# A chunk pair's added state products moved ahead of a tile of hidden products, with a filler behind them

## The chip, the cores and the metric

The kernel runs on one core of one Trainium2 chip. The metric is device time in microseconds, the median of several executions of the same program. Three executions of the kernel before took 361.55, 362.46 and 362.59 us.

## The reference

Two stages run one after the other. The first is a state-space recurrence over 768 tokens for 4 batches of 8 heads, with a state of 16 x 32 per head. In chunked form:

```
for each chunk:
    y_intra = ((C B^T) * L) x            # L: products of a, causal
    y_inter = (C state) * decay_to_i
    state   = decay_full * state + sum_j decay_from_j * B_j x_j
```

The sum in the last line is what this kernel calls the added products. The second stage takes y as 3072 tokens of 256 features through two layers with a leaky slope per hidden feature:

```
h = y @ w_in                              # 256 -> 2048
g = max(h, 0) + alpha * min(h, 0)
out = g @ w_out                           # 2048 -> 256
```

Everything is float32, except that the two weight matrices reach the kernel as float64 words, which it converts on the chip.

## The kernel before, in words

Tokens are taken in chunks of 128, two chunks making a pair, 12 pairs in all; four chunks make a group of 512 tokens for the second stage. The order of all work is written by hand: each engine runs its instructions in the order in which the code issues them, and waits for semaphores where a tile is not ready or not free.

The change lies in the start, `first_two()` (from line 816), which does the recurrence of pairs 0 and 1 while weights are still loaded and converted. It uses half chunks of 64 tokens. The steps of pair 1 that matter, with their lines:

- B and C of pair 1 are transposed on TensorE by `turned` (line 838), two transposes of B into one bank of PSUM, two of C into another; ScalarE copies both to SBUF, C first (line 840). `spread_c` (line 847, ScalarE) makes two masked copies of C, `decayed_c` (line 954, GpSimd) a decayed one.
- `scan` (line 864, VectorE) makes the decays, four of them, reading banks 0 to 3 of PSUM (`sp`).
- `added` (line 888, TensorE, 16 matmuls of 64 x 32, which are 32 records in the profile) makes the added products from `bn1` (B scaled, made on GpSimd at line 528) and `xt1` (x of pair 1, loaded by DMA at line 196). It writes the right-hand halves of the two banks `own`.
- `states` (line 903, VectorE) turns them into states, and `one_at_a_time` masks those on GpSimd (line 909).
- `gram_of` (line 874, TensorE) makes C B^T in banks 0 to 3, right-hand halves, and `times` (line 880, VectorE) multiplies it with the decays.
- `x_products` (line 922) and `state_products` (line 934) make y on TensorE, which `copy_out` (lines 942 and 943) brings to SBUF.

Beside these runs the second stage for group 0. `hidden_two` (line 1092) makes two tiles of hidden products for 256 tokens in one bank: four matmuls, two per tile, for the tile and half of the input features. It takes a function `after`, which is called behind each of the four and issues other work there; in `first_two` this is `among(i, k)`. So the added products stand behind the first of the four matmuls, gram behind the second, and the products of x and of the states behind the third. The four read columns 256 to 511 of w_in, the third and fourth tile of 128 hidden features. These columns are the second piece of w_in, whose conversion ends on GpSimd at line 327. Pair 0's y is their other operand.

`keep_warm` (line 335) issues fillers: matmuls of ones whose results nobody reads. There are four calls of it before the changed place.

Two banks are called `hp` (pool `ps_h`), two `ss` (`ps_s`), and four are named by number (`ps_q`). `second` is one of the `hp` banks; C's transposes go to it, and afterwards the tile of `hidden_two`.

Of the kernel before, what the change touches and what calls it, by code (L numbers as in the profile page):

```python
# [22 lines left out]
def kernel(  # L23
# [80 lines left out]
    def bank(i):  # L104


        return ps_q.tile([P, 512], F32, name="bank", tag=f"q{i}")
# [180 lines left out]
    def sign(dst, src, sg):  # L288

        if src.dtype == F32 or id(dst) in signs:  # L290
            return
        r = wtp.tile([P, 2, WQ], U32, name="wr")
        nc.vector.tensor_single_scalar(out=r, in_=parts[id(dst)][0], scalar=SIGN,
                                       op=ALU.bitwise_and)
        signs[id(dst)] = r
# [36 lines left out]
    def keep_warm(to, n, cols=2 * Q):  # L332

        for i in range(n):
            nc.tensor.matmul(to[:, :cols], warm.to_broadcast([P, P]), warm.to_broadcast([P, cols]),
                             start=True, stop=True, skip_group_check=True)
# [53 lines left out]
    def slope_signs():  # L390
        if moe_w_out.dtype == F32:
            nc.vector.tensor_single_scalar(out=s_out, in_=s_mul.bitcast(U32), scalar=SIGN,
                                           op=ALU.bitwise_and)
        else:
            for o, by in ((g_mul, 2.0**-11), (g_add, 2.0**25)):
                nc.gpsimd.tensor_scalar(out=o, in0=s_mul, scalar1=by, scalar2=None, op0=ALU.mult)
# [119 lines left out]
    def pair_loads(gp):  # L516

        b, c = divmod(2 * gp, CPB)
        nat, abc, xt, ap = loads["p", gp]

        bn = work.tile([P, 2, H * N], F32, name="bn")
        i, bi = divmod(b, 2)
        if gp >= HALF:
            pj = prt[i].rearrange("p (j b m h) -> p j b m h", j=2, b=2, h=H)[:, :, bi, c // 2]
        else:
            pj = (prt[i if gp >= NB else "short"]
                  .rearrange("p (b h c) -> p b c h", b=2, h=H)[:, bi, c : c + 2])
        nc.gpsimd.tensor_tensor(
            out=bn.rearrange("p k (h n) -> p k h n", h=H),
            in0=nat[:, 0].rearrange("p k (h n) -> p k h n", h=H),  # L530
            in1=pj.unsqueeze(3).to_broadcast([P, 2, H, N]), op=ALU.mult)
        return bn
# [8 lines left out]
    def spare():  # L541

        return ps_h.tile([P, GT], F32, name="hp", tag="hp")
# [272 lines left out]
    def first_two():  # L816
# [15 lines left out]
        def turned(nat, banks):  # L832


            bc = work.tile([P, 4, Q], F32, name="bc")
            for i, tp in enumerate(banks):
                for k in range(2):
                    nc.tensor.transpose(tp[:, k * P : (k + 1) * P], nat[:, i, k], ident)
            for i in (1, 0):
                nc.scalar.copy(out=bc[:, 2 * i : 2 * i + 2].rearrange("p k t -> p (k t)"),  # L840
                               in_=banks[i][:, : 2 * Q])
            return bc

        def spread_c(bc):
            cz = czp.tile([P, 2, 2, Q], F32, name="cz")
            for e in range(2):
                nc.scalar.mul(cz[:, e].rearrange("p k t -> p (k t)"),
                              bc[:, 2:].rearrange("p k t -> p (k t)"), par[:, e : e + 1])
            return cz
# [17 lines left out]
        def gram_of(bc, cz, banks):  # L867
            for v in range(2):
                for k in range(2):
                    for r in (2 * v, 2 * v + 1):  # L870
                        rs = slice(32 * r, 32 * r + 32)
                        for j, hs in enumerate(halves):
                            o = banks[r][hs, (2 + k) * Q : (3 + k) * Q]
                            nc.tensor.matmul(o.rearrange("p (e t) -> p e t", e=2), bc[rs, k, hs],
                                             cz[rs, :, k, hs], start=True, stop=True,
                                             tile_position=(32 * r, HQ * j),
                                             skip_group_check=True)

        def times(i, r, t):
            nc.vector.tensor_tensor(out=dec[i][:, r], in0=t[:, 2 * Q :], in1=dec[i][:, r],  # L880
                                    op=ALU.mult)

        def added(dps, bn, xt):
            for k in range(2):
                for r in range(4):
                    rs = slice(32 * r, 32 * r + 32)
                    for j, hs in enumerate(halves):
                        nc.tensor.matmul(dps[j][rs, k], bn[hs, k, rs],
                                         xt[hs, k, 2 * r * D : 2 * (r + 1) * D],
                                         start=True, stop=True, tile_position=(HQ * j, 32 * r),  # L890
                                         skip_group_check=True)

        def dps_in(banks):
            return [t[:, 2 * Q : 2 * Q + 4 * D].rearrange("p (k m) -> p k m", k=2) for t in banks]

        def states(i, dps, pf, cs=range(4)):
            for c in cs:
                if i == 0 and c == 0:
                    nc.scalar.copy(out=new[0][:, 0], in_=dps[0][:, 0])
                    continue  # L900
                e = (c + 1) * HQ - 1
                old = new[i][:, c - 1] if c else new[0][:, 3]
                nc.vector.scalar_tensor_tensor(out=new[i][:, c], in0=old, scalar=pf[:, e : e + 1],
                                               in1=dps[c % 2][:, c // 2], op0=ALU.mult,
                                               op1=ALU.add)

        def mask(i, cs):
            n = cs.stop - cs.start
            nc.gpsimd.tensor_tensor(
                out=sm[i][:, cs].rearrange("p k (g m) -> p k g m", g=2),  # L910
                in0=new[i][:, cs].unsqueeze(2).to_broadcast([P, n, 2, 2 * D]),
                in1=hmask.rearrange("p (g m) -> p g m", g=2).unsqueeze(1)
                .to_broadcast([P, n, 2, 2 * D]), op=ALU.mult)
# [24 lines left out]
        def copy_out(i, y):  # L938
            for w in range(KC):
                o = xts[0][:, w, 2 * i * Q : 2 * (i + 1) * Q].rearrange(  # L940
                    "p (k j t) -> p j k t", k=2, j=2)
                nc.scalar.copy(out=o[:, 0], in_=y[w][0])
                nc.scalar.copy(out=o[:, 1], in_=y[w][1])

        def places(first, second):
            return [[t[:, :Q].rearrange("p (k t) -> p k t", k=2) for t in ts]
                    for ts in (first, second)]

        def ss():
            return ps_s.tile([P, 512], F32, name="ss")  # L950

        def decayed_c(bc, pf):
            cd = work.tile([P, 2, Q], F32, name="cd")
            nc.gpsimd.tensor_tensor(out=cd.rearrange("p k t -> p (k t)"),
                                    in0=bc[:, 2:].rearrange("p k t -> p (k t)"), in1=pf,
                                    op=ALU.mult)
            return cd

        def one_at_a_time(i, cs):
            for c in cs:  # L960
                mask(i, slice(c, c + 1))
# [9 lines left out]
        sp = [bank(r) for r in range(4)]  # L971
# [5 lines left out]
        nat1, _, xt1, pf1 = loads["p", 1]  # L977
# [13 lines left out]
        dps = dps_in([hp, tp])  # L991
# [18 lines left out]
        sp = [bank(r) for r in range(4)]  # L1010
# [16 lines left out]
        bn1 = pair_loads(1)  # L1027
        convert_next(first=False)
        own = [ss(), ss()]
        second = spare()  # L1030
        bc1 = turned(nat1, (own[0], second))
        cz1 = spread_c(bc1)
        dps = dps_in(own)
        mask(0, slice(3, 4))
        slope_signs()
        cd1 = decayed_c(bc1, pf1)

        def among(i, k):
            if (i, k) == (0, 0):
                added(dps, bn1, xt1)  # L1040
                states(1, dps, pf1, range(3))
                one_at_a_time(1, range(3))
            if (i, k) == (0, 1):
                gram_of(bc1, cz1, sp)
                for r in range(4):
                    times(1, r, sp[r])
                states(1, dps, pf1, (3,))
                prelu_of[0]()
                convert_a(*pieces[2])
                sign(*pieces[2])  # L1050
            if (i, k) == (1, 0):
                y = places([own[0], bank(0)], [bank(1), bank(2)])
                x_products(y, xt1, 1)
                state_products(y, 1, cd1)
                copy_out(1, y)
# [507 lines left out]
```

## Time and profile before

| | us |
|---|---|
| median of three executions | 362.46 |
| lowest and highest | 361.55, 362.59 |
| the profiled execution, its own time | 361.22 |
| span of the profiled execution, first to last instruction | 359.5 |
| TensorE busy (products) | 352.6 (98%) |
| VectorE busy | 239.6 (67%) |
| GpSimd busy | 202.2 (56%) |
| ScalarE busy | 172.3 (48%) |
| mean granted clock of TensorE | 0.991 |
| TensorE waiting for the conversion of w_in, line 1092, longest | 1.2 |
| TensorE waiting at line 922, releaser "issue" | 1.1 |
| VectorE waiting for the added products, line 903 | 1.0 |

A busy TensorE is not TensorE at its peak, since products are pipelined and their ends are modelled. The profile names, for each idle stretch of an engine, what ended it: another engine's instruction, a DMA, or "issue", which means that the engine waited for nothing that the profile shows. A float32 matmul shows as two records, a transpose as one. The granted clock is the share of full speed that TensorE's clock had. Windows give, for a stretch of time, the busy microseconds of each engine and that clock. The chain of waits is followed back from the last instruction, and tells which engine's work set the end.

### The profile page before, as it was taken

Reading aid. Unit: us, or ns where it says so; the run is one execution under the profiler, and the core shown is the slowest. Engines: PE = TensorE matmul, PEld = TensorE weight load, DVE = VectorE, ACT = ScalarE, POOL = GpSimd, SP = SyncE. Lnnn points to the kernel's source line nnn. Section 1 sums busy time; section 2 is a strip of 40 time slices with the busy share of each in tenths; the row PEclk is TensorE's granted clock in tenths of the full one; section 3 lists DMA queues with packets and bytes.
Section 4 is the critical chain, followed back from the end, with each engine's and each line's share of the span. In section 5 each row is a group of like instructions: output and inputs, shape, how many; then the busy total and the mean of one; then the engine's idle time right before and its main releaser. Section 6 shows DMA issues by size and latency. Waiting matters only on the chain.

```text
span 359.5 us, 7769 instructions
## 1 busy us (share of the span) xinstructions
PE 352.6 (98%) x2981; PEld 286.4 (80%) x2981; DVE 239.6 (67%) x483; ACT 172.3 (48%) x391; POOL 202.2 (56%) x227
## 2 busy tenths in 40 slices
PE   8889999999999999999999999999999999999996
PEld 3567566668888888888888888888888888888885
DVE  6966996999947856866656856657856634643363
ACT  3537666535354445445345445445545444443431
POOL 6653748579847947536546536537536545434510
PEclk9988999999999999999999999999999999999999
DMA  8999999205436502502522521531201001001102
GB/s 149 189 211 339 253 282 204 77 2 116 131 86 145 110 3 60 116 3 49 101 61 51 94 64 43 97 69 42 34 2 31 0 2 29 2 1 29 33 0 58
DMA packets 105581, 30.24 MB, mean 84 GB/s; under 512 B 79896, under 2 KB 101448, under 8 KB 105544
## 3 DMA queue, kind: packets, MB, share of 16 engines
q1 hardware_dynamic: 103048, 29.43, 35.6%
q10 hardware_dynamic: 2496, 0.32, 0.6%
q8 instruction: 23, 0.38, 0.4%
q14 instruction: 14, 0.11, 0.1%
HBM read 26.32 MB, written 3.42 MB: 83 GB/s over the span
## 4 chain that ended last, share of the span: by engine, by line
PE 96%; DMA 1%; DVE 1%; issue 0%; POOL 0%; SPq 0%; ACT 0%; POOLq 0%
PE bank L1198 33%; PE hp L1223 28%; PE bank L1124 8%; PE hp L1077 6%; PE ss L1223 6%; PE hp L1092 2%; PE ss L782 1%; PE ss L726 1%; DMA nat<-in_B_dram 1%; PE bank L1191 1%; PE ss L800 1%; PE ss L774 1%; PE ss L737 1%; PE bank L1092 1%; PE ss L613 1%; PE ss L934 0%
## 5 line engine op out<-in xcount | busy, mean ns | idle before, releaser
L1280 POOL TENSOR_TENSOR gt<-gt 128x512 f32<-128x512 f32 x58 | 74.2, 1278 | 21.1 <-DVE gt L1208 16.3
L1198 PE MATMUL bank<-gt,w_out 128*128 128x256 f32 x320 | 83.5, 381 | 0.0
L1198 PEld LDWEIGHTS bank<-gt,w_out 128*128 128x128 f32 x320 | 60.1, 190 | 9.2 <-issue 1.0
L1208 DVE SCALAR_TENSOR_TENSOR gt<-hp,s_mul,gt 128x256 f32<-128x256 f32 x96 | 42.0, 479 | 29.1 <-ACT gt L1206 26.8
L1270 POOL TENSOR_TENSOR gt<-gt 128x512 f32<-128x512 f32 x20 | 25.4, 1269 | 62.6 <-DVE gt L1208 49.8
L1206 ACT ACTIVATE gt<-hp,s_alpha 128x256 f32<-128x256 f32 x96 | 40.3, 471 | 34.6 <-PE hp L1223 31.5
L1198 PE MATMUL bank<-gt,ws 128*128 128x256 f32 x224 | 55.9, 379 | 0.0
L1198 PEld LDWEIGHTS bank<-gt,ws 128*128 128x128 f32 x224 | 42.3, 190 | 5.6
L1223 PE MATMUL hp<-xs,w_in 128*128 128x256 f32 x160 | 41.9, 384 | 0.0
L1223 PE MATMUL hp<-xs,ws 128*128 128x256 f32 x160 | 41.2, 380 | 0.0
L1249 DVE TENSOR_TENSOR hp<-hp,u 128x512 f32<-128x512 f32 x20 | 14.0, 700 | 35.2 <-ACT u L1247 35.2
L1223 PEld LDWEIGHTS hp<-xs,ws 128*128 128x128 f32 x160 | 30.3, 190 | 4.3 <-POOL xs L1165 0.2
L1223 PEld LDWEIGHTS hp<-xs,w_in 128*128 128x128 f32 x160 | 29.7, 190 | 4.5
L1124 PE MATMUL bank<-w_out,gt 128*128 128x256 f32 x128 | 31.0, 384 | 0.0
L1124 PEld LDWEIGHTS bank<-w_out,gt 128*128 128x128 f32 x128 | 23.6, 190 | 6.5 <-issue 2.9
L1223 PE MATMUL ss<-xT,w_in 128*128 128x256 f32 x96 | 24.6, 379 | 0.0
L1077 PE MATMUL hp<-xT,w_in 128*128 128x512 f32 x48 | 22.7, 595 | 0.0
L556 DVE TENSOR_TENSOR_SCAN dec<-abc,bank 128x192 f32<-128x192 f32 x48 | 22.7, 523 | 0.0
L640 POOL TENSOR_TENSOR sm<-state,bmask 128x256 f32<-128x256 f32 (+1 forms) x10 | 6.2, 619 | 28.9 <-DVE state L637 28.9
L1238 ACT COPY m<-hp 128x512 f32<-128x512 f32 x8 | 4.7, 586 | 35.7 <-PE hp L1223 35.7
L1247 ACT COPY u<-hp 128x512 f32<-128x512 f32 x20 | 11.7, 585 | 19.4 <-PE hp L1223 19.4
L1208 DVE SCALAR_TENSOR_TENSOR gt<-c,s_mul,gt 128x256 f32<-128x256 f32 x40 | 20.6, 555 | 0.0
(230 smaller groups left out, 615.8 us busy)
## 6 DMA issues: line engine op xcount, KB each, us to landing
abc<-z SPq DMA_DIRECT2D x24, 192.0 KB
raw<-in_moe_w_in_dram SPq DMA_DIRECT2D x8, 512.0 KB
raw<-in_moe_w_out_dram SPq DMA_DIRECT2D x8, 512.0 KB
abc<-z SPq DMA_DIRECT2D x8, 512.0 KB
out_dram<-o_sb SPq DMA_DIRECT2D x32, 64.0 KB
nat<-in_B_dram SPq DMA_DIRECT2D x26, 64.0 KB
xt<-in_x_dram SPq DMA_DIRECT2D x12, 128.0 KB
xt<-in_x_dram SPq DMA_DIRECT2D x24, 64.0 KB
```

What stands on the lines that cost most here:

```text
L556: nc.vector.tensor_tensor_scan(out=dv[:, o : o + SQ], data0=abc[k][:, s : s + SQ], data1=ident_p[0][:, :SQ], initial=0.0, op0=ALU.mult, op ...
L1077: nc.tensor.matmul(hp, w_in[:, k, f * P : (f + 1) * P], xts[g][:, k], start=(k == 0), stop=(k == KC - 1))
L1092: nc.tensor.matmul(hp[:, i * nt : (i + 1) * nt], w_in[:, k, fs], xts[g][:, k, ts], start=(i == 0 and k == 0), stop=(k == KC - 1), skip_gro ...
L1124: nc.tensor.matmul(pos[0][t // 2][:, t % 2], gt[:, t * Q : (t + 1) * Q], w_out[:, f], start=(f == 0 and t % 2 == 0), stop=(f == NF - 1), s ...
L1198: nc.tensor.matmul(ms[g][i][:, h], w, blocks[g, z][n][:, p], start=(q == 0 and h == 0), stop=(q == NQ - 1), skip_group_check=True)
L1206: nc.scalar.mul(o[:, p], h[:, p], s_alpha[:, fs[p]])
L1208: nc.vector.scalar_tensor_tensor(out=o[:, p], in0=h[:, p], scalar=s_mul[:, fs[p]], in1=o[:, p], op0=ALU.mult, op1=ALU.max)
L1223: nc.tensor.matmul(to[:, p], w(2 * z + p), b, start=start and p == 0, stop=True, skip_group_check=True)
L1247: nc.scalar.copy(out=u2, in_=A)
L1249: nc.vector.tensor_tensor(out=Y, in0=Y, in1=u2, op=ALU.add)
L1270: nc.gpsimd.tensor_tensor(out=tc_, in0=g22, in1=g12, op=ALU.subtract)
L1280: eng.tensor_tensor(out=o, in0=x0, in1=x1, op=ALU.subtract)
```

## The change

Two things are changed, both in `first_two`, and one is added:

```diff
         own = [ss(), ss()]
         second = spare()
-        bc1 = turned(nat1, (own[0], second))
+        bc1 = turned(nat1, (sp[0], second))
         cz1 = spread_c(bc1)
         dps = dps_in(own)
         mask(0, slice(3, 4))
         slope_signs()
         cd1 = decayed_c(bc1, pf1)
+        added(dps, bn1, xt1)
+        states(1, dps, pf1, range(3))
+        one_at_a_time(1, range(3))
+        keep_warm(second, 1)

         def among(i, k):
-            if (i, k) == (0, 0):
-                added(dps, bn1, xt1)
-                states(1, dps, pf1, range(3))
-                one_at_a_time(1, range(3))
             if (i, k) == (0, 1):
                 gram_of(bc1, cz1, sp)
```

B of pair 1 is transposed into bank 0, which the first scan has read, instead of a bank of `own`. The added products, three of the four state updates and their masks are issued in front of the tile's first matmul instead of behind it. One filler of 256 columns is issued between the added products and the tile, into the bank that the tile takes next. On VectorE, ScalarE, GpSimd and SyncE the instructions keep their order. On TensorE the added products and the filler stand behind the transposes, and the tile's first two matmuls stand together; the program has one matmul more.

## Prediction

> **What bounds the kernel now.** I read the chain of waits first, then the 40 slices, then TensorE's timeline and one-microsecond windows around the moved step. The chain is TensorE for 96% of the span, so only time that TensorE gains or loses counts. Of the slices, one row matters:
>
> ```profile
> PEclk9988999999999999999999999999999999999999
> ```
>
> The granted clock is full except in the third and fourth slice (18 to 36 us), just behind the changed step. The timeline of TensorE there (start, duration, engine, line, tiles, count; the bracket is the idle time before it and what ended it):
>
> ```profile
> 16.29 0.38 PE L838 MATMUL hp<-ident,nat 128*128 128x128 f32 x2
> 17.87 0.70 PE L1092 MATMUL hp<-xT,w_in 128*128 128x256 f32 x2 [1.20 <-POOL w_in L327]
> 18.50 0.46 PE L888 MATMUL ss<-xt,bn 64*32 64x64 f32 x32
> 18.89 0.70 PE L1092 MATMUL hp<-xT,w_in 128*128 128x256 f32 x2
> 19.52 0.72 PE L874 MATMUL bank<-cz,bc 32*64 32x128 f32 x32
> 20.17 0.70 PE L1092 MATMUL hp<-xT,w_in 128*128 128x256 f32 x2
> ...
> 23.05 0.41 PE L922 MATMUL bank<-dec,xt 64*32 64x64 f32 x20 [1.05 <-issue]
> ```
>
> See two holes. The first, 1.20 us, waits for GpSimd's conversion of the second piece of w_in (16.55 to 17.81). The second, 1.05 us, stands inside the products of L922 and is released by "issue": nothing that the profile shows. After it the clock falls (windows: length, then busy time and counts of TensorE, weight loads, VectorE, ScalarE, GpSimd, then clock, DMA share, GB/s):
>
> ```profile
> 22.00:23.00 1.00, 0.00 (x0) 0.00 (x0) 0.94 (x3) 0.00 (x0) 0.00 (x0) 1.00 0.91 137
> 23.00:24.00 1.00, 0.95 (x28) 0.86 (x28) 0.90 (x3) 0.00 (x0) 0.11 (x1) 0.77 1.20 113
> 24.00:25.00 1.00, 1.00 (x12) 1.00 (x12) 1.00 (x2) 0.13 (x1) 1.00 (x1) 0.50 1.10 188
> 29.00:30.00 1.00, 1.00 (x3) 0.78 (x3) 0.62 (x1) 0.14 (x1) 0.23 (x1) 0.50 1.00 307
> 30.00:31.00 1.00, 1.00 (x5) 0.86 (x4) 0.27 (x1) 0.70 (x2) 1.00 (x1) 0.82 0.98 354
> ```
>
> Windows of 0.1 us put the fall at 23.57 and the return at 30.36: 6.79 us at half clock, some 3.4 us lost. So three things lie near the change: a hole that it fills, a hole that it does not touch, and a throttle.
>
> **What the Trainium skill says.** (1) "TensorE: Matmul & The Clock Gate", Part 1: the clock is halved or full, decided by how busy TensorE was in windows of about 3.4 us. The trace agrees in kind: 0.50 or 1.00, and 6.79 us is two such windows. (2) "Runtime: NRT & Kernel Launch", Instruction fetch mechanics: an engine's instructions are refilled in blocks of 256 (16 KiB), by a DMA queue of the sequencer's own. The page of before fits:
>
> ```profile
> q8 instruction: 23, 0.38, 0.4%
> ```
>
> That is 23 packets of 16 KB; 6041 TensorE instructions in the built program make 23.6 blocks. The 1.05 us hole stands after 706 of them (346 products and 346 weight loads in the windows up to 23.0, and 14 others in the program); 62 that run ahead of the program would put it on 3 x 256 (the 62 is inferred). One packet of this queue begins at 20.57 and lasts 1.04 us (6.5% of 16 engines over 20 to 21 us), so it ends at 21.6, and TensorE goes on at 23.05. I read the hole as a late instruction block. The block before ended at instruction 450, at 13.98, so the request is that old; from then on the 16 DMA engines were full (share 0.97 to 1.34 in each microsecond from 14 to 21). (3) "PSUM — Partial Sum Buffer", PSUM bank collisions: a bank may not be written by TensorE while another engine reads it. In the trace L888 comes only after both copies of L840 have ended (17.35).
>
> **The change part by part.** Sums are made against the profiled execution: 361.22 us, span 359.5, 1.7 around it; it stands 1.24 below the median 362.46 of the three timed runs (361.55 to 362.59). A difference carries over to the median.
>
> *B's transposes go to bank 0.* Same two instructions. They must wait for VectorE's scan of that bank, over at 14.14, against 16.07 when they run; ScalarE's copy (16.97) waits for the same scan. Cost nothing. The gain is that the added products need not wait for ScalarE's copies.
>
> *The added products (32 matmul records, L888) move ahead of the tile, into the first hole.* They need bn, made by 15.40, and pair 1's x, whose DMAs were issued from 13.44 to 14.65. Its landing isn't shown; before, L888 at 18.50 did not wait for it. Early end: they run at 16.7, right behind the transposes. Late end: 18.5. I take 16.7 to 17.1, since the DMA engines had moved some 345 KB from 13.4 to 16.2, more than the 320 KB of C and x.
>
> *The filler, one 256-column product into the bank of the tile.* A lone one costs 0.70 (L335 at 13.37). It waits for ScalarE's copy of C, 16.71 to 17.08, and so ends at about 17.8, as the conversion does (17.81): it costs 0 to 0.1, hidden by GpSimd. If x lands at 18.5, it and L888 delay the tile by 1.7 us.
>
> *TensorE then:* first product of the tile at 17.87, as before, since GpSimd still bounds it. Its second product follows back to back: 0.70 + 0.43 (two records at 0.216, as L1124's eight in 1.73 on the chain) instead of 0.70 + 0.39 + 0.63, saving 0.59. Gram, the third product: 17.87 + 1.13 + 0.65 + 0.63 = 20.28, where before it was 20.87.
>
> *VectorE:* the three state updates of L903 waited 0.95 for L888 and ran 19.13 to 20.11; now they follow the scans at 18.17 and end at 19.15. The order of VectorE's queue stays, so nothing is put behind a new wait. The four products of L880 (1.42) no longer start at 20.22 but when half of gram is done, 19.0 + 0.33 + 0.1, and end at 20.85 instead of 21.64. Nor do GpSimd's masks (L909) get later. SyncE's queue and all DMAs stay.
>
> *Where it goes:* L922 starts at 20.28 and no longer stops for VectorE. 42 of its 64 records, at 0.41/20 each as in the row at 23.05, take it to the block's end: 21.1 instead of 21.99, so TensorE is 0.9 us early at the second hole. Three instructions more ahead of L922 move that end by two records, nothing else. But the block it waits for was requested at 13.98, before the first instruction that moves, and sits behind DMAs issued before 17.5, which the change doesn't touch. So it should arrive at 23.05 all the same. What is late next is the fetch: the hole grows from 1.05 to about 2.0 us and swallows the 0.9. Even the late end of x (L922 at about 22) is mostly covered by it.
>
> *From 23.05 on* nothing is new: 22 records instead of 20 (0.04), the state products, the copies, the last product of the tile, and eleven to twelve products at half clock if the throttle stays. Sum: about 0, which gives 362.4.
>
> **Rivals.**
> 1. *The hole moves with TensorE* (it isn't a DMA's landing, or the fetch comes earlier): -0.9, 361.6. For: "issue" names no releaser. Against: its place on 256 instructions, the packet at 20.57.
> 2. *The clock doesn't fall.* The filler and L888 fill a hole of 1.2 us within the 6.8 us before the fall (16.74 to 23.57). Avoided whole, it gives half of 6.79: -3.4, 359.1; cut to one window, -1.7, 360.7. For: the filler is a full-width product, and 16.74 to 20.15 was only 2.28 of 3.41 us busy. Against: the later window, 20.15 to 23.57, was 2.35 of 3.42 us busy and gets emptier, about 1.5, by my own account of the hole.
> 3. *Slower: the clock falls a window earlier or returns a window later,* because of that emptier window. 3.4 us more at half clock cost up to 1.7: 364.1; half that where part of it lies in the hole. It decides once the window up to 23.57, or one that straddles the hole otherwise, is too empty for the clock to come back after the next: of 3.4 us the hole would take 2.0. Against: L922 and the state products are short and would cost little at half clock.
> 4. *x lands late and the filler delays the tile:* up to +0.3 behind the hole, 362.7.
>
> **How the numbers follow.** Likeliest, the hole swallows it and the clock behaves as before: 0.48, 362.4, with the runs' own spread 361.6 to 363.1. The hole moves: 0.12. Clock kept throughout: 0.07; for one window: 0.10. Slower by the clock: 0.17. Late x: 0.06. A measurement of this kernel tells from no change about 0.3%, 1.1 us. Faster by more: 0.17 and 0.03 from the moving hole's edge, 0.20. Slower: 0.17 and 0.01 of late x, 0.18. Same: 0.62. The range takes in the one-window gain, 360.6, and the nearer half of the slower case, to 363.8; it leaves out 0.07 below and about 0.09 above.
>
> **What would show it.** L888 in the changed profile at 16.7 to 17.1, the wait of L1092 for GpSimd shrunk to about 0.1, L880 ending near 20.9, the "issue" hole beginning near 21.1 and ending near 23.05, the clock at 0.50 from about 23.6 for two windows. I am wrong if the hole ends earlier or keeps its 1.05 us, if L888 waits for a DMA past 17.4, or if the time at half clock isn't near 6.8 us.

## The result and the profile after

The changed kernel takes 364.51 us, the median of 8 executions (362.6 to 365.44). The kernel before, executed beside it 8 times, takes 361.99 us. The ratio is 1.0062, with a 95% interval of 1.0034 to 1.0090: slower, by 2.5 us between the medians and 2.2 us by the ratio, and outside the predicted range. The profiled execution took 364.29 us (before: 361.22), with a span of 362.6 us (359.5).

First the place of the change, on TensorE's timeline of the changed kernel:

```profile
17.84 0.45 PE L888 MATMUL ss<-xt,bn 64*32 64x64 f32 x32
18.37 0.70 PE L335 MATMUL hp<-const-float32-1.0 128*128 128x256 f32 x2
19.11 1.13 PE L1092 MATMUL hp<-xT,w_in 128*128 128x256 f32 x4
20.17 0.72 PE L874 MATMUL bank<-cz,bc 32*64 32x128 f32 x32
...
23.81 2.43 PE L1092 MATMUL hp<-xT,w_in 128*128 128x256 f32 x10
```

The steps stand in the predicted order, without the hole of 1.20 us, and there is no "issue" hole inside L922 at all. Everything lies some 1.2 us later than predicted, because in this execution the clock fell early, from 7.3 to 10.7 us. That part of the program is untouched, and two profiles of kernels with the old order (e4 and e11 below) show the same fall. Still, the next row of products, L1092 x10, runs at 23.81 and takes 2.43 us. Before, it ran at 25.19 and took 4.63, since the clock stood at half there. By TensorE's product L624 the changed kernel is 3.9 us ahead (33.61 against 37.52). The gain is made, and more than it. Then it is lost in one place, which VectorE's timeline of the changed kernel shows (the bracket is the idle time before the instruction, and what ended it):

```profile
40.28 0.28 DVE L637 SCALAR_TENSOR_TENSOR state<-gt,ap,ss 128x64 f32<-128x64 f32 x1 [4.91 <-DMA ap<-pf]
40.48 2.41 DVE L562 TENSOR_TENSOR_SCAN dec<-abc,bank 128x256 f32<-128x256 f32 x4
...
43.93 0.74 DVE L1081 SCALAR_TENSOR_TENSOR gt<-hp,s_mul,gt 128x512 f32<-128x512 f32 x1
```

and the same stretch of VectorE's timeline before:

```profile
39.26 0.28 DVE L637 SCALAR_TENSOR_TENSOR state<-gt,ap,ss 128x64 f32<-128x64 f32 x1 [0.16 <-DMA ap<-pf]
39.46 2.41 DVE L562 TENSOR_TENSOR_SCAN dec<-abc,bank 128x256 f32<-128x256 f32 x4
```

L637 is the first state update of pair 2. It needs `ap`, the decay products of that pair: VectorE computes them (line 439), a DMA writes them to DRAM (`pf`, line 442), and another reads them back spread over the partitions (line 167). Before, VectorE reached L637 at about 39.1 us and stood 0.16 us for `ap`. After, it reached it at about 35.4 and stood 4.91 us. `ap` itself was not sooner, but 1.0 us later. Behind L637 in VectorE's queue stand the scans L562 and the product L1081 at 43.93, which frees a bank of PSUM for TensorE. On TensorE's timeline after:

```profile
41.27 0.38 PE L737 MATMUL ss<-cz,bc 32*128 32x256 f32 x2
44.73 0.72 PE L737 MATMUL hp<-cz,bc 32*128 32x256 f32 x1 [3.08 <-DVE gt L1081]
```

TensorE stands for 3.08 us, a hole that the kernel before has not. There L737 follows the products in front of it with no idle time:

```profile
43.05 1.88 PE L1077 MATMUL hp<-xT,w_in 128*128 128x512 f32 x4
...
44.88 0.48 PE L737 MATMUL hp<-cz,bc 32*128 32x256 f32 x1
```

Windows of the changed kernel (length, then busy time and counts of TensorE, weight loads, VectorE, ScalarE, GpSimd, then clock, DMA share, GB/s) show what follows it:

```profile
43.00:44.00 1.00, 0.00 (x0) 0.00 (x0) 0.90 (x3) 0.00 (x0) 0.00 (x0) 1.00 0.70 107
44.00:45.00 1.00, 0.27 (x4) 0.27 (x8) 1.00 (x3) 0.00 (x0) 0.84 (x1) 0.92 0.20 32
45.00:46.00 1.00, 1.00 (x9) 0.85 (x6) 1.00 (x3) 0.00 (x0) 0.92 (x2) 0.50 0.26 42
...
51.00:52.00 1.00, 1.00 (x3) 0.53 (x2) 0.21 (x1) 0.00 (x0) 0.64 (x1) 0.67 1.12 327
```

TensorE has nothing to do at 43, and from about 44.8 to 51.7 the clock is at half. The kernel before had its 6.8 us at half clock from 23.57 to 30.36, ahead of the wait; in this execution of the changed kernel they come behind it, where nothing hides them. The chain of waits of the changed kernel, no longer TensorE's alone, goes through the two transfers (start, duration):

```profile
27.13 8.51 DMA pf<-rpf
35.66 4.54 DMA ap<-pf
```

The 8.51 us are not all travel of a small write. The DMA engines are full then: over 27 to 40 us, the main queue took this share of the 16 engines (packets, MB, the time that the packets took as a share of 16 engines' span) in the changed kernel

```profile
q1 hardware_dynamic: 3772, 4.01, 95.6%
```

and before

```profile
q1 hardware_dynamic: 4043, 4.54, 104.0%
```

Both also issue in one queue, SyncE's. The column behind the start is how long the issue itself took, in the changed kernel

```profile
27.13 0.93 SPq L442 DMA_DIRECT2D pf<-rpf  x1
28.11 4.32 SPq L160 DMA_DIRECT2D abc<-z  x2
32.53 2.96 SPq L254 DMA_DIRECT2D raw<-in_moe_w_out_dram  x1
35.66 0.61 SPq L167 DMA_DIRECT2D ap<-pf  x1
```

and before

```profile
27.00 0.84 SPq L442 DMA_DIRECT2D pf<-rpf  x1
27.89 2.88 SPq L160 DMA_DIRECT2D abc<-z  x2
30.88 2.96 SPq L254 DMA_DIRECT2D raw<-in_moe_w_out_dram  x1
34.01 0.60 SPq L167 DMA_DIRECT2D ap<-pf  x1
```

The write of `pf` goes out at the same time, 27.1 against 27.0. Behind it stand 1 MB of spread decays (`abc`) and 512 KB of weights, whose issue crawls, and only then is `ap` asked for.

### The profile page after: what moved, and what is told of

Read it like the earlier page. It is cut to its first block, busy times and chain, and to the rows that moved or that the text cites. A ratio compares the mean times of both kernels' runs of the same rounds, so it can differ in the third digit from the quotient of the medians.

```text
span 362.6 us, 7773 instructions
## 1 busy us (share of the span) xinstructions
PE 354.0 (98%) x2983; PEld 286.6 (79%) x2983; DVE 238.1 (66%) x483; ACT 172.1 (47%) x391; POOL 203.1 (56%) x227
## 3 DMA queue, kind: packets, MB, share of 16 engines
HBM read 26.32 MB, written 3.42 MB: 82 GB/s over the span
## 4 chain that ended last, share of the span: by engine, by line
PE 90%; DMA 5%; DVE 3%; ACT 1%; SPq 0%; issue 0%; DVEq 0%
PE bank L1198 33%; PE hp L1223 28%; PE bank L1124 7%; PE ss L1223 6%; PE hp L1077 4%; DMA pf<-rpf 2%; PE ss L782 1%; DMA ap<-pf 1%; PE ss L726 1%; DMA nat<-in_B_dram 1%; PE bank L1191 1%; PE ss L800 1%; PE ss L774 1%; PE hp L737 1%; PE ss L737 1%; DVE dec L562 1%
## 5 line engine op out<-in xcount | busy, mean ns | idle before, releaser
L1124 PE MATMUL bank<-w_out,gt 128*128 128x256 f32 x128 | 32.8, 400 | 0.0
L1124 PEld LDWEIGHTS bank<-w_out,gt 128*128 128x128 f32 x128 | 24.8, 199 | 7.1 <-issue 3.9
```

Source lines behind the costliest of these rows:

```text
L1124: nc.tensor.matmul(pos[0][t // 2][:, t % 2], gt[:, t * Q : (t + 1) * Q], w_out[:, f], start=(f == 0 and t % 2 == 0), stop=(f == NF - 1), s ...
```

## The experiments

**The theories.** T, the wait for `ap`: the time at which pair 2 can start on VectorE is set by the DMA engines and SyncE's queue, not by TensorE. What TensorE gains upstream becomes a longer wait there, and where TensorE's hole behind it is long, the clock falls as well. The rivals: the throttle falls more often for another reason, the filler above all; the added products' new place costs something by itself, at the instruction block; or the two times differ by chance.

A measure used below: half-clock windows per execution, (1 - mean clock) x 2 x span / 3.41 us, rounded. It comes from the clock and span of each timed run, so it has more behind it than one profile.

**e1: the changed kernel without the filler.**

```diff
-        keep_warm(second, 1)
```

> The changed kernel without its one filler; the added products stay in front of the tile. Theory T (transfers set the end of the start): in the changed profile the clock stayed up at 23.6 us, TensorE came 3.9 us early to the products near 34 us, and VectorE then waited 4.9 us for pair 2's decay products (ap), with TensorE behind it. Without the filler the clock should fall near 23.6 again, TensorE comes late, nothing waits for ap, and the time is that of before, 362.0 within 0.8; if the added products alone hold the clock up, it is that of the changed kernel, 364.5, with the wait in it. Rival L (the moved order or the filler itself costs time at its own place): about 0.4 to 0.7 less than the changed kernel, 363.9, with the wait for ap still there.

Measured: 363.03 us against 361.97, ratio 1.0026 [1.0002, 1.0050]. Its profile has VectorE's wait for `ap` at 6.20 us, a hole of 3.41 us in TensorE before L737, and the clock at half from 43.4 to 53.7; it is one of the longest executions of this kernel (365.92 us). The median lies between the expected values, with the wait still there. So a loss stays without the filler. It is smaller than with it (0.26% against 0.62%, and 0.33% in e5), but the intervals overlap: a share of the filler in the loss is neither shown nor excluded. The profile also shows when pair 1's x lands: the second half of L888 waits for it until 17.30.

**e2: the kernel before with the filler alone.**

```diff
         cd1 = decayed_c(bc1, pf1)
+        keep_warm(second, 1)
```

> The kernel before with the one filler put in front of the tile, and nothing else of the change. Theory T: if the filler is what holds the clock up, this kernel is slow as the changed one, 364.0 to 365.0, with a TensorE hole of about 3 us near 41 to 44 us and half clock behind it. Rival L (the moved added products cost): as before, 362.0. If the hole inside the products of x stays at 1 us or more and the clock falls near 23.6, theory T gives 362.0 too.

Measured: 362.08 us, 1.0011 [0.9992, 1.0030]. In the old order the filler costs nothing that can be measured. But in this profile L637 waits 3.98 us for `ap`, and TensorE stands for 1.96 us before L737, although the added products are in their old place. So the wait does not belong to the changed order alone.

**e3 and e4: `ap` asked for sooner, in the changed kernel and in the one before.** The same move in both puts the load ahead of one piece of weights on SyncE's queue:

```diff
     hidden_two(0, 0, 2 * Q, spare())()
+    load_products(NB, loads["p", NB][3])
     convert_next(first=False)
-    load_products(NB, loads["p", NB][3])
```

> The changed kernel with one DMA issue moved: pair 2's decay products (ap) are asked for in front of one 512 KB load of w_out instead of behind it, which held SyncE for 2.96 us. Theory T: ap lands up to 3 us sooner, near 37 us, VectorE's wait of 4.9 shrinks to 2 or less, TensorE's hole of 3.1 near 41 us closes, the clock doesn't fall behind it, and the time drops by 3 to 5 us against the changed kernel, to 359.5 to 361.5. Rival L: no change, 364.5. Rival R (the early fall of the clock at 7 us, chance alone, made the difference): 364.5 less what chance gives, no change in the hole.

> The kernel before with the same DMA issue moved and nothing else. Theory T: nothing waited for ap there (0.16 us), TensorE was late by its half clock, so 362.0 within 0.5. A rival, that the earlier ap is a gain by itself: 359 to 360.

Measured: the changed kernel 361.91, 0.9991 [0.9969, 1.0012], and the one before 360.38, 0.9943 [0.9923, 0.9964]. This brings the changed kernel level with the kernel before as it was, though not to the 359.5 to 361.5 that I had expected. Between the two orders, each with `ap` sooner, 1.5 us remain, and the intervals of the two ratios don't meet. I had expected the kernel before to stay at 362.0, and it became 1.6 us faster: that expectation missed, and it says more than a hit would have. The earlier `ap` is a gain at equal numbers of half-clock windows too (with none, a median of 359.25 us against 361.23; with one, 360.53 against 362.26). The wait for `ap` had bound the kernel before too, then, in most executions, and the 0.16 us in its profile is a tie and no sign of slack. In e4's profile the wait is even longer than before, and yet pair 2 starts earlier (VectorE):

```profile
38.70 0.28 DVE L637 SCALAR_TENSOR_TENSOR state<-gt,ap,ss 128x64 f32<-128x64 f32 x1 [2.73 <-DMA ap<-pf]
```

**e5: the changed kernel once more,** on another chip, as the partner of the next two.

> The changed kernel once more, beside the others of this group. In the six profiles so far the span is the start of VectorE's first state update of pair 2 (L637, released by the landing of ap) plus 320.0 to 320.2 where the clock doesn't fall behind it, and plus 322.3 to 322.7 where it does. Theory T: L637 again waits several us for ap and starts near 40 to 41, TensorE stands near 41 to 45 us, span 360 to 363.5 by that sum; the median stays 363.5 to 364.5. Rival R (chance): median within 0.8 of before, 362.

Measured: 364.32 us against 362.76, 1.0033 [1.0012, 1.0054]. So the loss is there again, somewhat smaller, and chance alone, which would have given 362 within 0.8, is out. Its profiled execution is a quick one (span 360.1, `ap` waited for 3.60 us, hole before L737 1.58 us, no fall behind it), and here the "issue" hole does stand:

```profile
17.73 1.13 PE L1092 MATMUL hp<-xT,w_in 128*128 128x256 f32 x4
...
22.15 0.42 PE L922 MATMUL bank<-dec,xt 64*32 64x64 f32 x22 [0.82 <-issue]
23.71 2.50 PE L1092 MATMUL hp<-xT,w_in 128*128 128x256 f32 x5
```

**e6 and e7: useless work for TensorE ahead of the wait.** Four fillers of 512 columns, in the changed kernel and in the one before. If TensorE's time counts, they cost their length; if T holds, they cost nothing and close the hole.

```diff
-    rest = hidden_two(0, 2, 2 * Q, bank(3))
+    third = bank(3)
+    keep_warm(third, 4, GT)
+    rest = hidden_two(0, 2, 2 * Q, third)
```

> The changed kernel with four fillers of 512 columns (some 3.4 us of TensorE for nothing at full clock) put between the two tiles of the second half, near 26 us. Theory T: the end of the start is set by ap, so delaying TensorE costs nothing; the fillers take the place of its wait near 41 us, the clock has no hole to fall behind, and the time goes down by up to 2.5, to 361.5 to 362.5. Rival L (TensorE's own chain sets the end): up by 3.4, to 367 to 368.

> The kernel before with the same four fillers. Theory T: in executions whose clock falls near 23.6 us TensorE and ap come at the same time, so the fillers (some 3.4 us, more while at half clock) cost most of their length; in those whose clock stays up they cost nothing. A median of 362.5 to 364.5. Rival L: 362.0 plus 3.4, 365.4, in all.

Measured: the changed kernel 362.91, 1.0004 [0.9984, 1.0025], which is 1.4 us faster than e5 beside it by the medians and 1.0 by the means. The kernel before: 362.44, 1.0006 [0.9984, 1.0027]. Rival L, which asked for 367 to 368 and 365.4, is excluded. TensorE's timeline of e6:

```profile
28.13 3.61 PE L335 MATMUL bank<-const-float32-1.0 128*128 128x512 f32 x8
31.58 1.89 PE L1092 MATMUL bank<-xT,w_in 128*128 128x256 f32 x8
...
46.46 0.48 PE L737 MATMUL hp<-cz,bc 32*128 32x256 f32 x1
```

The fillers take 3.45 us (28.13 to 31.58), and L737 has no hole. 3.45 us of work for nothing made one kernel faster and cost the other nothing that its median shows. In most executions TensorE's own work in the first 40 us therefore doesn't set the end, although the chain of waits of before is TensorE for 96%. The half-clock windows per execution say why the changed kernel got faster: 2.05 in e5, 0.68 in e6. At equal numbers of windows the fillers are not free: with one window 363.28 us against 362.67 (e6 and e5) and 363.29 against 362.68 (e7 and before), with two 364.24 against 364.26 and 364.87 against 362.88. All of this is less than their length. And with the fillers the two orders no longer differ (1.0004 and 1.0006).

**e8: before, with `ap` sooner and the write of `pf` from ScalarE's queue.**

```diff
-        nc.sync.dma_start(out=scratch["pf", 0], in_=rpf)
+        nc.scalar.dma_start(out=scratch["pf", 0], in_=rpf)
```

> The kernel before with ap asked for in front of the load of w_out, as in e4, and with the write that ap reads back (pf) issued from ScalarE's queue instead of SyncE's, where it stood behind five loads of weights. Theory T: pf is written some 1 to 3 us sooner, ap lands near 35 to 37, L637 starts by then, and the span is that plus 320, or what TensorE's own chain sets, near 356.5 to 357.5: a time of 358.2 to 359.5, below the 360.4 of e4. Rival: SyncE still waits for the write, and the loads queued before hold it as long: 360.4 as e4.

Measured: 360.80 us, 0.9938 [0.9913, 0.9962], the gain of e4 and no more, as the rival said. `ap` is issued at 31.28 us, but its issue takes 3.71 us, and L637 runs at 39.25.

**e9 and e10: `ap` ahead of the spread decays too,** before and changed. The rows' scan and its products move into the function `among`, behind `states(1, dps, pf1, (3,))`, and the load goes in front of `abc`:

```diff
                 states(1, dps, pf1, (3,))
+                held["pr"] = rows_scan(0)
+                rows_products()
...
-        held["pr"] = rows_scan(0)
-        rows_products()
+        load_products(NB, loads["p", NB][3])
         load_spread(2, *divmod(4, CPB))
```

> The kernel before with the two scans that make the decay products of all pairs done right behind pair 1's last state, so that their write (pf) stands in front of the last load of weights, and with ap asked for in front of the decays' spread (abc). Theory T: ap lands some 3 to 6 us sooner than in before (39.2), so that L637 starts when TensorE's products or abc allow, 34 to 37 us, and the span is that plus 320: a time of 356 to 359. If SyncE now stands at the wait for pf and the loads behind it come late, ap is early and abc late, and the scans behind L637 wait instead: 360 to 362. Rival L: no change, 362.

> The same with the changed order. Theory T: with ap out of the way the change is at last worth what it saved at its place, 0.5 to 1.0 us where TensorE's products bind, so 355.5 to 358.5 and not above e9; its loss against before is gone. If the change has a cost of its own, it stays 1 to 2 us above e9.

Measured: 359.59, 0.9935 [0.9911, 0.9959], from 7 executions, and 360.42, 0.9956 [0.9935, 0.9977]. e9 is faster than both kernels of this case, though it misses the 356 to 359 of the expectation. e10 misses its own, 355.5 to 358.5 and not above e9: it is 0.8 us slower than e9, which the overlapping intervals leave open. SyncE's queue in e9:

```profile
27.08 0.42 SPq L442 DMA_DIRECT2D pf<-rpf  x1
27.60 0.63 SPq L254 DMA_DIRECT2D raw<-in_moe_w_in_dram  x1
32.82 0.60 SPq L167 DMA_DIRECT2D ap<-pf  x1
33.47 1.08 SPq L160 DMA_DIRECT2D abc<-z  x2
```

and VectorE's timeline there:

```profile
35.98 0.27 DVE L637 SCALAR_TENSOR_TENSOR state<-gt,ap,ss 128x64 f32<-128x64 f32 x1
37.94 2.42 DVE L562 TENSOR_TENSOR_SCAN dec<-abc,bank 128x256 f32<-128x256 f32 x4 [1.69 <-DMA abc<-z]
```

The wait for `ap` is gone, and what is late next is `abc`, in e10 too (1.98 us of waiting, the first scan at 39.47), so that a gain on TensorE can't come through there either. The write of `pf` still goes out at 27.08, so the gain is from the order behind it, not from the earlier scan.

**e11: before, with both small transfers of `ap` from ScalarE's queue,** and the load of `ap` moved in front of that of w_out, as in e4.

```diff
-        nc.sync.dma_start(out=ap, in_=rows.unsqueeze(1).to_broadcast([H, N, 2 * Q]))
+        (nc.scalar if gp == NB else nc.sync).dma_start(
+            out=ap, in_=rows.unsqueeze(1).to_broadcast([H, N, 2 * Q]))
...
-        nc.sync.dma_start(out=scratch["pf", 0], in_=rpf)
+        nc.scalar.dma_start(out=scratch["pf", 0], in_=rpf)
```

> The kernel before with both the write of pf and the load of ap issued from ScalarE's queue, ap in front of the load of w_out. Theory T: off SyncE's queue they don't stand behind the loads of weights; ap lands near 32 to 36, L637 starts by 36 to 37, a time of 357 to 359. ScalarE stands at the wait for pf's landing, though, and what it holds up (the scaled halves of the tiles) may cost 1 to 3 us: then 360 to 362.

Measured: 361.50 us, 0.9969 [0.9951, 0.9988], half of what the order on SyncE's queue gives. The Trainium skill, "DMA: Bandwidth & Descriptors", Issuing engines are not separate DMA queues, says that DMAs of several issuing engines run on the same 16 DMA engines and interleave there, so that another issuer saves the time of issuing only. The trace agrees: the write of `pf`, issued by 27.31 us from ScalarE, lets `ap` be asked for at 32.72, 5.4 us later; in e9 it is 5.3 us (27.50 to 32.82) from SyncE. And the wait for that write now stands in ScalarE's queue, in front of its work for the second stage:

```profile
32.72 1.18 ACTq L167 DMA_DIRECT2D ap<-pf  x1
33.94 0.84 ACT L1103 ACTIVATE gt<-bank,s_alpha 128x256 f32<-128x256 f32 x2 [3.42 <-issue]
```

ScalarE stands for 3.42 us, and VectorE 3.38 us behind it at line 1114, so that L638 (L637 elsewhere) starts only at 40.99, though it doesn't wait for `ap` at all.

**e12: the changed kernel with `ap` sooner and no filler.** What remains between e3 and e4, 1.5 us, was to be told apart.

```diff
-        keep_warm(second, 1)
```

> The changed kernel with the decay products of pair 2 loaded ahead of the weights, once more, now without the filler behind the added products. With the filler this came to 361.9, 1.5 us above the kernel before with the same early load (360.4). If the filler is what remains (it delays the tile, or shifts the throttle's windows): 360.4 to 360.9. If it is the order of the added products itself: 361.5 to 362.2. The first scan of pair 2 starts at 38 to 39 us, and the span is 319.8 more, plus 0.3 to 2.5 where the clock falls behind that scan.

Measured: 360.95 us against 361.75, 0.9988 [0.9965, 1.0011], from 14 executions. The ratio is that of e3, while the median is 1.0 us lower and lies at the edge of the filler's range: not decided, neither for the filler nor against it.

**The table that holds it together.** From the profile of each kernel: the wait of L637 for `ap`, the start of the first scan L562 of pair 2, the span less that start, and TensorE's hole before L737. Then, from the timed runs, half-clock windows per execution, and the time. The profiled execution is one of those runs and can lie far from their median (365.92 us in e1, 359.6 in e3, 361.84 in e5):

| kernel | wait for ap | first scan | span less it | hole | windows | median us |
|---|---|---|---|---|---|---|
| before | 0.16 | 39.46 | 320.0 | none | 1.1 to 1.5 | 361.75 to 362.76 |
| after | 4.91 | 40.48 | 322.1 | 3.08 | 2.25 | 364.51 |
| e5, after again | 3.60 | 40.35 | 319.8 | 1.58 | 2.05 | 364.32 |
| e1, no filler | 6.20 | 41.73 | 322.5 | 3.41 | 1.67 | 363.03 |
| e6, after, late fillers | 1.27 | 42.16 | 319.7 | none | 0.68 | 362.91 |
| e7, before, late fillers | 0.96 | 40.58 | 319.8 | none | 0.86 | 362.44 |
| e2, before, filler | 3.98 | 41.42 | 319.8 | 1.96 | 1.00 | 362.08 |
| e3, after, ap sooner | 0.89 | 38.09 | 319.8 | none | 1.55 | 361.91 |
| e12, the same, no filler | 3.52 | 38.50 | 320.4 | 1.50 | 1.50 | 360.95 |
| e11, both from ScalarE | none | 41.18 | 319.8 | none | 0.90 | 361.50 |
| e8, pf from ScalarE | 1.08 | 39.45 | 319.8 | none | 0.38 | 360.80 |
| e10, after, early rows | 1.58 | 39.47 | 320.3 | 1.90 | 0.76 | 360.42 |
| e4, before, ap sooner | 2.73 | 38.90 | 319.8 | 0.89 | 0.77 | 360.38 |
| e9, before, early rows | none | 37.94 | 319.8 | none | 0.71 | 359.59 |

Read the fourth column first. In nine of the fourteen profiles the span is the start of that scan plus 319.7 to 319.8 us, whatever was done ahead of it. It is more in five: four whose clock falls behind the wait (after and e1 for two and three windows, e10 and e12 for one), and the kernel before with 320.0. In before, TensorE comes to L737 5.4 us behind the scan (44.88); in e6 it is 4.3. From that I infer that TensorE was some 0.2 us late in before, and so that no gain on TensorE ahead of that place could be worth more than this there.

## Why the prediction was wrong

**What held.** The local steps came as worked out, best seen in e5, which has no early fall of the clock. The added products run at 16.46 (predicted 16.7 to 17.1; the transposes ahead of them are 0.15 us earlier as well), the tile's two products back to back from 17.73 (17.87), and gram's third product at 19.44, so that it ends near 20.1 (20.28). VectorE's products L880 follow half of gram and end at 20.98 (20.85). x is seen to land at 17.30 in e1 and 17.13 in e12, inside its bounds and without delay for the tile, and by about 16.7 in e5, where L888 does not stop for it. (The DMA engines had moved some 380 KB from 13.4 to 16.2 us, not 345; the conclusion is the same.) The filler is hidden in after, e3 and e5, where the tile starts 0.05 us behind the conversion of w_in. In e6 and e10, where the added products run later, it holds the tile up by some 0.4 and 0.5 us.

**The instruction block: half right.** It was to land at 23.05 whatever TensorE did, so that the hole would grow to about 2.0 us. The place was right: behind the hole stand 20 records in before, e1, e7, e8, e9, e11 and e12, which lack the filler, and 22 in e2, e3, e5, e6 and e10, which have it, as the two records of the filler demand. That supports the reading as a block of instructions. The time was not right: with the changed order the hole ends at 22.02 to 22.84 us and is 0.40 to 0.99 us long (e1, e3, e5, e6, e10, e12), against 22.82 to 23.75 and 0.24 to 1.61 with the old one (before, e2, e7, e8, e9, e11). The queue's packet began at 19.8 to 20.4 us with the changed order, and at 20.5 to 21.4 with the old (but 16.1 in e4, which has no hole). Why it came sooner isn't shown. In the profiled execution of after it began at 20.0, and TensorE, late from the early fall of the clock, came after it: so no hole. Rival 1 was nearer, then: the products behind (L1092 x10) start at 23.4 to 24.3 us with the changed order and at 24.2 to 25.2 with the old one, a true gain on TensorE of some 0.9 us by the means (23.8 and 24.7), as that rival had it.

**The step that failed is "From 23.05 on nothing is new", with its premise, that the chain is TensorE for 96%, "so only time that TensorE gains or loses counts".** What lay behind was not neutral. The transfer of `ap` landed at 39.26 us in before, level with VectorE's coming there, and nothing in the change moves it earlier. A gain of 0.9 us ahead of it could only become a wait (4.91, 3.60 and 6.20 us in after, e5 and e1). These waits are longer than 0.9 us because before came to L637 late, behind 6.79 us at half clock; an execution that was at half clock there for one window only waits in the old order too (3.98 us in e2). None of the four rivals had this transfer. A chain of waits names one releaser at each step, and where two arrive together the other isn't seen. The line that showed it was in the profile of before: L637 with 0.16 us of waiting for a DMA.

**The loss, then, is the throttle's, in another place than rival 3 put it.** That rival's size, 364.1 us, was near by luck: it too was a window more at half clock, but it sat in the hole at L922. There the clock did better than forecast in after, and no fall followed, as rival 2 had it; in e5, e3 and e6, with the same order, it fell there for one window. The hole that counts is the new one before L737. Of the 3.1 us between the two profiled spans, 1.0 is the later scan (40.48 for 39.46) and 2.1 is what lies behind it (322.1 for 320.0), the clock at half from 44.8 to 51.7. That the scan was later is not shown to be the change's doing (it was at 41.42 in e2). In before, the fall at 23.57 lies ahead of the wait for `ap`, which covers all but some 0.2 us of it in that execution. Over the timed runs, executions of e5 with one half-clock window had a median of 362.67 us and of before 362.68; with two, 364.26 and 362.88. So with one window there is no difference, and two cost 1.4 us more in the changed kernel; it also has more of them, 2.05 a run against 1.36. (No execution of e5 had none; those of before took 361.52, so a first window costs time there too.) e6 is the test of it: with TensorE kept busy the windows go to 0.68 a run, and the loss goes too, against before and against e7, the old order with the same fillers.

**What stays open.** The wait explains where the gain went, and the fall behind it most of the loss of the profiled execution. Where the clock falls in the changed kernel is known for its two profiled executions only (after, e5); that the second window of its other runs lies behind the wait is inferred. With `ap` sooner, the changed order is still slower than the old one (e3 against e4, 1.5 us; e10 against e9, 0.8, inside the noise). So the landing of `ap` explains why there was no gain, and not the whole difference between the two orders. The changed order has more half-clock windows in the first of these pairs (1.55 and 0.77) but not in the second. A cost of its own of the added products' new place is not excluded there, though e6 and e7 show none, and e1 and e12 did not tell whether the filler has a part in it.

## What to carry to other kernels

Before a gain on the busiest engine is booked, look downstream for the next transfer that some engine waits for, however short that wait is: a wait of 0.16 us is a tie, and a tie caps the gain. What is saved ahead of a fixed landing turns into idle time of the very engine that was sped up, which can cost its clock; the remedy is to ask for the small transfer ahead of the large ones in its queue (e4 and e9, 1.6 and 2.4 us), not to hurry the engine. Useless work put ahead of a suspected wait (e6, e7) is a cheap test of who sets the end.

## What the runs showed of the hardware

*The throttle's falls vary in place and in number.* They began near 7 us (after, e4, e11), at 23 to 25 (before, e2, e3, e5, e6, e8), behind the wait at 43 to 45 (after, e1, e10, e12), or did not come (e7, e9), and timed runs of one kernel have none to three windows. "TensorE: Matmul & The Clock Gate", Part 1, says that the window runs freely and does not start with the kernel, so that its phase varies from run to run; that fits. Of the holes before L737, those of 3.08 and 3.41 us were followed by a fall of two and three windows, those of 1.50 and 1.90 by one, and those of 1.96, 1.58 and 0.89 by none: length alone doesn't decide.

*The falls keep to a grid.* In each profile the changes of the clock lie whole multiples of 3.41 us apart (stretches at half clock of 3.41, 6.83 and 10.24 us). Cut each profile into steps of 3.41 us from such a change, and compare the same place of the program. In six profiles a step ends at 7.1 to 7.4 us: TensorE was busy for 2.15, 2.28 and 2.37 us of it in e4, e11 and after, where the clock then fell, and for 2.39, 2.45 and 2.46 in e6, e10 and e2, where it did not. At the hole before L737 the step ahead of the fall had 0.33, 1.51, 1.91 and 2.18 us (after, e10, e12, e1); where no fall came, the emptiest step had 2.41, 2.53 and 2.60 us (e2, e4, e5). The hole of 1.50 us in e12 lay inside one step (40.00 to 43.41), the one of 1.96 us in e2 across two (they meet at 44.67). So where a hole falls on the grid counts beside its length. No one share holds for every place: 2.12 us in e11 (34.74 to 38.15) brought no fall, 2.57 us in e5 (19.89 to 23.30) did.

*A small transfer is slow among large ones.* The 48 KB of `pf` had landed, as seen from the issue of `ap`, for which SyncE stood idle, 5.3 us behind the end of its own issue in e9 and 6.4 in e10 (28.00 to 34.45). In e3, e4 and e12, where the 1 MB of `abc` was asked for in between, it was 5.8, 7.5 and 7.0 us. The 128 KB of `ap` was there 4.6 us behind its issue in before (34.61 to 39.26), where 1.5 MB had been issued between `pf` and it, and 2.2 us in e10 (35.05 to 37.21), where 0.5 MB had.
